# Turning the second tile's keys and queries behind the second product, not around it

## The chip, the core and the metric

The kernel runs on one core of a Trainium2 chip. The metric is the device time of one execution in microseconds (us), lower is better. Times are medians of several executions; the profile is one execution, recorded by the hardware profiler.

## The reference

Local attention feeds two feed-forward layers. Only the first part matters here; cut to it:

```python
# q, k, v: 4 batches, 8 heads, 768 positions, 64 features; 8 memory keys and values per head
for c in range(24):                            # chunks of 32 queries, context 16 left, 8 right
    scores = q_c @ concat(mem_k, k_ctx).T / 8
    a = softmax(scores)
    out[:, :, c_start:c_end] = a @ concat(mem_v, v_ctx)
x = out as 3072 tokens x 512
x = softplus(x @ w_in) @ w_out                 # d_ff 2048
x = (x @ w_a) * (x @ w_b) @ w_o2               # d_ff 1536
```

## The kernel before

The 3072 tokens are eight tiles of 384. For each tile the kernel computes attention, then for each of 16 slices f of d_ff the product `ph` (x with a slice of w_in, `emit_h`, L539), the softplus (`emit_soft`: three ACT instructions L545 to L547 make `e`, DVE adds `g` at L549, `split` makes the high part `g_h` on ACT, L526, and the low part `g_l`, L529, on DVE in the first tile), and two slices later the product `px` with w_out (`emit_x1`, L562), which adds into the four banks acc0 to acc3. Each matrix product is done as three, of high and low halves. The second layer follows when all tiles are done.

The first tile is the place of the change. Its attention is done ahead (`blocks`, written out by the table ROUND). Weights come from HBM as raw 64-bit words by `fetch_to(n)`, which requests all raws up to number n on SP's queue (L101). Each is converted by `Weight`: `top` on ACT (L116), `value` on DVE (two instructions, L121 and L122), `high` on ACT (L127), `low` on DVE (L130). Raws 0 to 5 are converted within ROUND, the others within the slices of the first tile, two half steps at a time (`convert`).

The second tile's first attention unit needs its keys and queries with features on partitions. `Packed(1).load(half)` requests them in two halves of four heads (`kp`, 400 KB, `qp`, 384 KB, and 8 KB of memory keys), and `Packed(1).turn(i)`, four calls, turns a pair of heads each: PE multiplies with the identity into `ptk` (L287, bank acc{i}) and `ptq` (L293, one of the two "att" banks), ACT copies `ptk` to `kn` (L289), DVE copies `ptq` to `qn` (L295). The scores `sc` of the unit (L304, L305) read `kn` and `qn` and take the two "att" banks after them.

Everything in the first tile stands in the order in which the program writes it, on each engine. Within slice f the order is: `ph`, softplus with conversions, plan entries of slots up to 2f, `px` of slice f - 2, plan entries of slots up to 2f + 1:

```python
plan += [(at, -1, lambda i=i: packed[1].turn(i)) for i, at in enumerate(PACKED_AT)]
def att_at(slot):
    while plan and plan[-1][0] <= slot:
        plan.pop()[2]()
```

The scores of the second tile's first unit stand at slot 5, behind the first `px`.

Of the kernel before, what the change touches and what calls it, by code (L numbers as in the profile page):

```python
# [31 lines left out]
ROUND = ((2, "normal"), (4, "place"), (None, "top"), (0, "scores"), (1, "soft"), (None, "low"), (None, "value"),  # L32
         (2, "flip"), (3, "values"), (None, "high"))
EARLY_RAW = (2, 3, 4, 5, 6, 6)
PACKED_AT = (0, 0.1, 2, 2.1)
AHEAD = 6
FILL = {(2, "scores"): 1, (2, "flip"): 5, (3, "flip"): 4, (3, "values"): 1, (4, "scores"): 2, (4, "flip"): 1,
        (4, "values"): 1, (5, "scores"): 2, (5, "flip"): 1, (5, "values"): 1, (6, "flip"): 4, (6, "values"): 1,
# [2 lines left out]
ROUNDS_CV = 6  # L41
# [9 lines left out]
def attn_moe_moe2(ctx: ExitStack, tc: tile.TileContext, q, k, v, mem_k, mem_v,  # L51
# [85 lines left out]
    def fetch1(n):  # L137
        dst, f = uses[n]
        if dst is w1:
            fetch(w1, f, w_in[:, f * P:(f + 1) * P].rearrange("(k p) f -> p k f", p=P))  # L140
        else:
            fetch(w1o, f, w_out[f * P:(f + 1) * P, :])
# [357 lines left out]
    for i, unit in enumerate(units[UPT:]):  # L500
# [10 lines left out]
        if i % UPT == UPT - 1 and unit.u + 1 < len(units):  # L511
            turned = at + steps[0][0] - steps[-1][0]
            plan += [(turned + 1 + part, i, partial(loaded.fetch, unit.u // UPT + 1, part)) for part in range(KT)]
    plan += [(at, -1, lambda i=i: packed[1].turn(i)) for i, at in enumerate(PACKED_AT)]
    plan.sort(key=lambda p: p[:2])
# [311 lines left out]
    def order():  # L827
# [6 lines left out]
        def fetch_to(n):  # L834
            nonlocal n_w1
            while n_w1 < min(n, len(uses)):
                fetch1(n_w1)
                n_w1 += 1
# [5 lines left out]
        for i in range(BPT):  # L844
            blocks[i].load()
            fetch_to(EARLY_RAW[i])
        packed[1] = Packed(1)
        packed[1].load(0)
        fetch_to(ROUNDS_CV + 2)
        packed[1].load(1)  # L850
        fetch_to(ROUNDS_CV + AHEAD)
        weights = [Weight(*use) for use in uses]
# [141 lines left out]
        while jobs:  # L994
# [6 lines left out]
            else:  # L1001
                next_job()

    order()


# [28 lines left out]
```

## Time and profile before

| what | value |
|---|---|
| median of 3 executions | 1189.81 us (1187.59 to 1191.05) |
| profiled execution | 1187.76 us |
| its span, first to last instruction | 1185.7 us |
| PE (matmul) busy | 1177.1 us, 99% |
| DVE busy, ACT busy | 734.8 us (62%), 536.7 us (45%) |

The profiled execution's time is 2.06 us over its span. PE is busy nearly all of the span, DVE and ACT over the whole kernel are not; in the first 100 us they are busy 81.03 and 80.98 us of it.

### The profile page before, as it was taken

The page shows a single profiled execution, that of the slowest core. Times are in us where ns is not written, and L with a number is a line of the kernel's source. Part 1 is how long each engine was busy: PE and PEld are TensorE (multiplying, and loading weights), DVE is VectorE, ACT ScalarE, POOL GpSimd, SP SyncE. Part 2 cuts the span into 40 slices and gives each one's busy share as a digit, 9 for nine tenths or more (in the row PEclk, how much of TensorE's full clock was granted, in tenths as well). Part 3 has the DMA queues.
Part 4 walks back from the last instruction along what each step waited for, and adds up shares of the span by engine and source line. Part 5 has one row for each costly group of instructions (what it writes and reads, how often), then busy time and mean ns, then how long its engine had stood idle before and what let it go on. Part 6 is the DMA issues. An engine that isn't in the chain of part 4 may idle for free.

```text
span 1185.7 us, 21520 instructions
## 1 busy us (share of the span) xinstructions
PE 1177.1 (99%) x7966; PEld 1115.3 (94%) x7966; DVE 734.8 (62%) x1707; ACT 536.7 (45%) x1329; POOL 279.2 (24%) x249
## 2 busy tenths in 40 slices
PE   9999999999999999999999999999999999999998
PEld 7899999999999999999999999999999999999997
DVE  6888654555546555465387668755666456655565
ACT  6899665655656566565564433221112201212010
POOL 2000323223232222322325778200211002100000
PEclk9999999999999999999999999999999999999999
DMA  9955334353343533432556895788554965379521
GB/s 232 296 183 112 107 86 111 93 113 107 85 110 93 118 110 83 105 97 62 177 206 239 321 339 193 266 323 301 201 196 143 375 231 184 133 254 365 198 80 54
DMA packets 198841, 209.86 MB, mean 177 GB/s; under 512 B 121632, under 2 KB 150224, under 8 KB 198736
## 3 DMA queue, kind: packets, MB, share of 16 engines
q1 hardware_dynamic: 198352, 208.43, 54.8%
q8 instruction: 63, 1.03, 0.4%
q14 instruction: 42, 0.34, 0.1%
q0 software_dynamic: 384, 0.05, 0.0%
HBM read 158.11 MB, written 50.33 MB: 176 GB/s over the span
## 4 chain that ended last, share of the span: by engine, by line
PE 95%; DMA 2%; SPq 2%; ACT 0%; DVE 0%; issue 0%; DVEq 0%
PE px L562 23%; PE ph L539 22%; PE py L749 17%; PE pW L726 8%; PE pX L726 8%; PE pV L726 8%; PE pY L726 4%; PE pxa L476 2%; PE sc L429 1%; DMA kp<-in_k_dram 1%; DMA raw<-in_moe_w_in_dram 1%; SPq L330 1%; SPq L327 0%; SPq L101 0%; PE sc L304 0%
## 5 line engine op out<-in xcount | busy, mean ns | idle before, releaser
L539 PE MATMUL ph<-x,w 128*128 128x384 f32 x1536 | 289.9, 336 | 0.1
L539 PEld LDWEIGHTS ph<-x,w 128*128 128x128 f32 x1536 | 266.7, 188 | 2.5 <-issue 0.3
L749 PE MATMUL py<-w2o,c 128*128 128x512 f32 (+1 forms) x870 | 222.2, 392 | 0.0
L549 DVE SCALAR_TENSOR_TENSOR g<-ph,e 128x384 f32<-128x384 f32 x128 | 71.3, 557 | 206.3 <-ACT e L547 205.9
L749 PEld LDWEIGHTS py<-w2o,c 128*128 128x128 f32 x870 | 160.5, 188 | 25.3
L808 ACT CAST c<-c 128x384 fp32r<-128x384 f32 x48 | 24.7, 514 | 302.5 <-DVE c L806 269.8
L726 PE MATMUL pX<-x,u 128*128 128x384 f32 x576 | 115.5, 334 | 0.0
L758 DVE TENSOR_TENSOR y<-py,y 128x512 f32<-128x512 f32 (+1 forms) x121 | 83.0, 686 | 47.4 <-PE py L749 46.9
L545 ACT ACTIVATE e<-ph 128x384 f32<-128x384 f32 x128 | 62.2, 486 | 104.0 <-PE ph L539 90.0
L726 PEld LDWEIGHTS pX<-x,u 128*128 128x128 f32 x576 | 102.1, 188 | 4.1
L447 DVE STREAM_TRANSPOSE af<-sm 32x256 f32<-32x256 f32 x180 | 78.2, 435 | 2.5
L804 DVE TENSOR_TENSOR d<-pW,q 128x384 f32<-128x384 f32 x48 | 26.7, 557 | 68.5 <-PE pW L726 68.5
L546 ACT ACTIVATE e<-e 128x384 f32<-128x384 f32 x128 | 67.3, 526 | 4.0
L547 ACT ACTIVATE e<-e 128x384 f32<-128x384 f32 x128 | 67.3, 526 | 3.8
L383 ACT ACTIVATE sm<-sm,st 128x96 f32<-128x96 f32 x168 | 60.5, 362 | 3.6 <-DVE st L379 3.6
L818 ACT CAST c<-c 128x384 fp32r<-128x384 f32 x48 | 24.6, 513 | 77.9 <-DVE c L816 76.9
L726 PE MATMUL pW<-xs,u 128*128 128x384 f32 x288 | 57.8, 335 | 0.0
L726 PE MATMUL pV<-xx,u 128*128 128x384 f32 x288 | 57.8, 335 | 0.0
L726 PE MATMUL pV<-xs,u 128*128 128x384 f32 x288 | 57.6, 334 | 0.0
L726 PE MATMUL pW<-xx,u 128*128 128x384 f32 x288 | 57.6, 334 | 0.0
L726 PE MATMUL pY<-xs,u 128*128 128x384 f32 x288 | 57.6, 334 | 0.0
L726 PEld LDWEIGHTS pV<-xx,u 128*128 128x128 f32 x288 | 51.5, 188 | 4.2
(251 smaller groups left out, 2228.9 us busy)
## 6 DMA issues: line engine op xcount, KB each, us to landing
u<-u_scratch SPq DMA_DIRECT2D x108, 512.0 KB
u_scratch<-u SPq DMA_DIRECT2D x36, 512.0 KB
w2o<-w2o_scratch SPq DMA_DIRECT2D x36, 512.0 KB
u<-u_scratch SPq DMA_DIRECT2D x36, 256.0 KB
raw<-in_moe_w_in_dram SPq DMA_DIRECT2D x16, 512.0 KB
raw<-in_moe_w_out_dram SPq DMA_DIRECT2D x16, 512.0 KB
vn<-in_v_dram SPq DMA_DIRECT2D x35, 176.0 KB
raw_a<-in_moe_w_a_dram SPq DMA_DIRECT2D x12, 512.0 KB
```

Source lines behind the costliest of these rows:

```text
L383: nc.scalar.activation(sm[:, h], sm[:, h], AF.Exp, bias=st[:, 0, h:h + 1], scale=-1.0, accum_out=st[:, 1, h:h + 1])
L447: nc.vector.transpose(out=af[32 * kb:32 * kb + 32, x], in_=self.sm[32 * x:32 * x + 32, :, 32 * kb:32 * kb + 32])
L539: nc.tensor.matmul(ph, lhsT=a, rhs=c, start=n == 0, stop=n == 3 * KT - 1)
L545: nc.scalar.activation(e, ph, AF.Abs)
L546: nc.scalar.activation(e, e, AF.Exp, scale=-1.0)
L547: nc.scalar.activation(e, e, AF.Ln, bias=1.0)
L549: nc.vector.scalar_tensor_tensor(g, ph, 0.0, e, ALU.max, ALU.add)
L562: nc.tensor.matmul(acc[t][i][:, :TT], lhsT=a, rhs=c, start=f == 0 and m == 0, stop=f == NF1 - 1 and m == 2)
L726: nc.tensor.matmul(bank[:, :TT], lhsT=u[:, j, a, kt * P:kt * P + P], rhs=x[:, c, kt, :], start=first_ and m == 0, stop=m == 3 * KH - 1, sk ...
L749: nc.tensor.matmul(b, lhsT=c[:, x, r], rhs=w[:, y, cols], start=n == 0, stop=n == 3 * GROUP - 1)
L758: tt(y, b, y, ALU.add)
L804: tt(d21, w[:, :TT], q, ALU.add)
```

## The change

The four turns move from slots 0, 0.1, 2, 2.1 to 2, 2.1, 3, 3.1. A turn with a fractional slot is taken at the next whole one: before, the first two stood at slots 0 and 1, between the first and the second `ph`, and the others at slots 2 and 3, between the second and the third. Now the first stands at slot 2 and the next two at slot 3, between the second and the third `ph`, and the fourth at slot 4, behind the third. The requests of raws 6 and 7 are put ahead of the first half's keys and queries, and that of raw 8 ahead of the second half's.

```diff
-PACKED_AT = (0, 0.1, 2, 2.1)
+PACKED_AT = (2, 2.1, 3, 3.1)
...
         for i in range(BPT):
             blocks[i].load()
             fetch_to(EARLY_RAW[i])
+        fetch_to(ROUNDS_CV + 2)
         packed[1] = Packed(1)
         packed[1].load(0)
-        fetch_to(ROUNDS_CV + 2)
+        fetch_to(ROUNDS_CV + 3)
         packed[1].load(1)
         fetch_to(ROUNDS_CV + AHEAD)
```

On PE, from the first tile's first `ph` on (ptk_0 and ptq_0 are the first turn, ptk_3 and ptq_3 the fourth), the program before had this:

```order
L539 MATMUL ph_0_623<-x_429,w_320 128x384 x12
L287 MATMUL ptk_0_673<-ident,kp_0_173 64x104 x8
L293 MATMUL ptq_0_683<-ident,qp_0_174 64x128 x6
L287 MATMUL ptk_1_691<-ident,kp_0_173 64x104 x8
L293 MATMUL ptq_1_701<-ident,qp_0_174 64x128 x6
L539 MATMUL ph_1_709<-x_429,w_368 128x384 x12
L287 MATMUL ptk_2_747<-ident,kp_1_183 64x104 x8
L293 MATMUL ptq_2_757<-ident,qp_1_184 64x128 x6
L287 MATMUL ptk_3_769<-ident,kp_1_183 64x104 x8
L293 MATMUL ptq_3_779<-ident,qp_1_184 64x128 x6
L539 MATMUL ph_2_787<-x_429,w_424 128x384 x12
```

Now it has this, with the first `px` next in both:

```order
L539 MATMUL ph_0_623<-x_429,w_320 128x384 x12
L539 MATMUL ph_1_673<-x_429,w_368 128x384 x12
L287 MATMUL ptk_0_711<-ident,kp_0_177 64x104 x8
L293 MATMUL ptq_0_721<-ident,qp_0_178 64x128 x6
L287 MATMUL ptk_1_733<-ident,kp_0_177 64x104 x8
L293 MATMUL ptq_1_743<-ident,qp_0_178 64x128 x6
L287 MATMUL ptk_2_751<-ident,kp_1_185 64x104 x8
L293 MATMUL ptq_2_761<-ident,qp_1_186 64x128 x6
L539 MATMUL ph_2_769<-x_429,w_424 128x384 x12
L287 MATMUL ptk_3_806<-ident,kp_1_185 64x104 x8
L293 MATMUL ptq_3_816<-ident,qp_1_186 64x128 x6
```

The second product has moved ahead of the first two turns, and the fourth turn behind the third product.

On DVE, from the low half of weight 8 on (tmp is the value of a raw, w the low half of a weight), the program before had this:

```order
L130 TENSOR_TENSOR w_670<-tmp_650,w_670 128x512
L295 COPY qn<-ptq_0_683 128x384
L295 COPY qn<-ptq_1_701 128x384
L121 TENSOR_SCALAR tmp_727<-raw_193 128x512
L122 SCALAR_TENSOR_TENSOR tmp_727<-raw_193,tmp_727 128x512
L549 SCALAR_TENSOR_TENSOR g_1_734<-ph_1_709,e_1_730 128x384
L130 TENSOR_TENSOR w_736<-tmp_663,w_736 128x512
L529 TENSOR_TENSOR g_1l<-g_1_734,g_1h 128x384
L121 TENSOR_SCALAR tmp_744<-raw_195 128x512
L122 SCALAR_TENSOR_TENSOR tmp_744<-raw_195,tmp_744 128x512
L295 COPY qn<-ptq_2_757 128x384
L295 COPY qn<-ptq_3_779 128x384
```

Now it has this:

```order
L130 TENSOR_TENSOR w_670<-tmp_650,w_670 128x512
L121 TENSOR_SCALAR tmp_691<-raw_193 128x512
L122 SCALAR_TENSOR_TENSOR tmp_691<-raw_193,tmp_691 128x512
L549 SCALAR_TENSOR_TENSOR g_1_698<-ph_1_673,e_1_694 128x384
L130 TENSOR_TENSOR w_700<-tmp_663,w_700 128x512
L529 TENSOR_TENSOR g_1l<-g_1_698,g_1h 128x384
L121 TENSOR_SCALAR tmp_708<-raw_195 128x512
L122 SCALAR_TENSOR_TENSOR tmp_708<-raw_195,tmp_708 128x512
L295 COPY qn<-ptq_0_721 128x384
L295 COPY qn<-ptq_1_743 128x384
L295 COPY qn<-ptq_2_761 128x384
L130 TENSOR_TENSOR w_786<-tmp_691,w_786 128x512
```

Five steps (a value, g of slice 1, a low half, its low part g_1l, a value) have moved ahead of the first copy of a turn. The fourth copy, qn from ptq_3, now stands behind this piece, which follows the last row above:

```order
L130 TENSOR_TENSOR w_786<-tmp_691,w_786 128x512
L549 SCALAR_TENSOR_TENSOR g_2_793<-ph_2_769,e_2_789 128x384
L121 TENSOR_SCALAR tmp_796<-raw_636 128x512
L122 SCALAR_TENSOR_TENSOR tmp_796<-raw_636,tmp_796 128x512
L529 TENSOR_TENSOR g_2l<-g_2_793,g_2h 128x384
L130 TENSOR_TENSOR w_803<-tmp_708,w_803 128x512
```

Before, no copy stood behind those rows; the softmax of the unit followed them, as it now follows the fourth copy.

On SP's queue, behind the last load of the first tile's values, the requests before were these (raw_179 is raw 6, raw_181 raw 7, raw_189 raw 8, raw_191 raw 9):

```order
L274 DMA kp_0_173<-in_k_dram 100x4x256
L275 DMA kp_0_173<-in_mem_k_dram 2x4x256
L276 DMA qp_0_174<-in_q_dram 128x4x192
L101 DMA raw_179<-in_moe_w_in_dram 128x4x256
L101 DMA raw_181<-in_moe_w_out_dram 128x1024
L274 DMA kp_1_183<-in_k_dram 100x4x256
L275 DMA kp_1_183<-in_mem_k_dram 2x4x256
L276 DMA qp_1_184<-in_q_dram 128x4x192
L101 DMA raw_189<-in_moe_w_in_dram 128x4x256
L101 DMA raw_191<-in_moe_w_out_dram 128x1024
```

Now they are these (raws 6, 7 and 8 are raw_173, raw_175 and raw_183):

```order
L101 DMA raw_173<-in_moe_w_in_dram 128x4x256
L101 DMA raw_175<-in_moe_w_out_dram 128x1024
L274 DMA kp_0_177<-in_k_dram 100x4x256
L275 DMA kp_0_177<-in_mem_k_dram 2x4x256
L276 DMA qp_0_178<-in_q_dram 128x4x192
L101 DMA raw_183<-in_moe_w_in_dram 128x4x256
L274 DMA kp_1_185<-in_k_dram 100x4x256
L275 DMA kp_1_185<-in_mem_k_dram 2x4x256
L276 DMA qp_1_186<-in_q_dram 128x4x192
L101 DMA raw_191<-in_moe_w_out_dram 128x1024
```

Raws 6 and 7 now stand ahead of both halves, raw 8 between them, and raw 9 where it was.

## Rows read from the trace of the kernel before

**Rows 1.** The page: busy time by engine; granted clock in tenths, 40 slices.

```profile
PE 1177.1 (99%) x7966; PEld 1115.3 (94%) x7966; DVE 734.8 (62%) x1707; ACT 536.7 (45%) x1329; POOL 279.2 (24%) x249
...
PEclk9999999999999999999999999999999999999999
```

**Rows 2.** Waits of PE over the whole span, all there are: us, times, longest.

```profile
PE pat L355 <- ACT x L369: 2.6, 3, 1.3
PE fill L492 <- POOL mem_n L228: 1.3, 1, 1.3
PE ptq L293 <- DVE qn L295: 1.0, 1, 1.0
```

**Rows 3.** Timeline of PE, 37 to 55 us: start, us, what, [idle before <-releaser].

```profile
37.06 2.64 PE L539 MATMUL ph<-x,w 128*128 128x384 f32 x12
...
39.63 0.93 PE L287 MATMUL ptk<-ident,kp 104*64 104x104 f32 x16
...
42.53 2.36 PE L539 MATMUL ph<-x,w 128*128 128x384 f32 x12
...
44.81 0.93 PE L287 MATMUL ptk<-ident,kp 104*64 104x104 f32 x16
...
46.77 0.88 PE L293 MATMUL ptq<-ident,qp 128*64 128x128 f32 x12 [1.02 <-DVE qn L295]
...
47.48 0.89 PE L287 MATMUL ptk<-ident,kp 104*64 104x104 f32 x16
...
48.95 2.35 PE L539 MATMUL ph<-x,w 128*128 128x384 f32 x12
...
53.31 0.40 PE L304 MATMUL sc<-kn,qn 64*64 64x88 f32 x8
...
54.56 2.35 PE L539 MATMUL ph<-x,w 128*128 128x384 f32 x12
```

**Rows 4.** Timeline of ACT, 40 to 52 us.

```profile
40.74 0.71 ACT L116 ACTIVATE raw<-raw 128x512 f32<-128x512 f32 x1 [1.49 <-DMA raw<-in_moe_w_in_dram]
...
41.87 0.47 ACT L545 ACTIVATE e<-ph 128x384 f32<-128x384 f32 x1
...
43.36 0.66 ACT L116 ACTIVATE raw<-raw 128x512 f32<-128x512 f32 x1
...
51.34 0.49 ACT L545 ACTIVATE e<-ph 128x384 f32<-128x384 f32 x1
```

**Rows 5.** Timeline of DVE, 37 to 56 us.

```profile
37.38 0.42 DVE L121 TENSOR_SCALAR tmp<-raw 128x512 uint32<-128x512 uint32 x1
...
38.51 0.42 DVE L121 TENSOR_SCALAR tmp<-raw 128x512 uint32<-128x512 uint32 x1
...
43.49 0.56 DVE L549 SCALAR_TENSOR_TENSOR g<-ph,e 128x384 f32<-128x384 f32 x1 [0.70 <-ACT e L547]
...
45.56 0.69 DVE L130 TENSOR_TENSOR w<-tmp,w 128x512 fp32r<-128x512 f32 x1
...
46.16 1.01 DVE L295 COPY qn<-ptq 128x384 f32<-128x384 f32 x2
...
47.10 0.42 DVE L121 TENSOR_SCALAR tmp<-raw 128x512 uint32<-128x512 uint32 x1
...
50.97 1.02 DVE L295 COPY qn<-ptq 128x384 f32<-128x384 f32 x2
...
55.66 0.25 DVE L379 CUSTOM_DVE_ANT_0 sm<-sc,mask 128x96 f32<-128x96 f32 x1
```

**Rows 6.** Window 40 to 42 us: busy PE, PEld, DVE, ACT, POOL, PEclk, DMA share, GB/s.

```profile
40.00:42.00 2.00, 2.00 (x48) 2.00 (x45) 1.27 (x3) 1.26 (x3) 0.00 (x0) 1.00 1.10 377
```

**Rows 7.** Timeline of PE, 0 to 31 us.

```profile
1.29 3.78 PE L492 MATMUL fill<-mem_n 128*128 128x512 f32 x4 [1.29 <-POOL mem_n L228]
...
27.84 1.13 PE L492 MATMUL fill<-ident 128*128 128x512 f32 x2
...
30.28 0.61 PE L355 MATMUL pat<-ident,work 128*96 128x128 f32 x4 [1.31 <-ACT x L369]
```

## The prediction

> **What bounds the kernel now.** I read the page first: PE is busy 99% of the span and its granted clock is full in every slice [rows 1]. So the time is PE's work plus PE's waits, and a change that adds no matmuls can move the end only through the waits. The list of PE's waits is the second view: it has three lines, and the last one, 1.0 us on a copy of the turned queries, is the only one within the change [rows 2]. No later wait is listed. The reader should see two things in this. At most about 1 us can be won here. And whatever PE loses before about 55 us it cannot win back, because behind that point no wait is left to shorten; a shift there goes through to the end.
>
> The third view is PE's timeline. From 39.63 PE does turns 0 and 1, the second `ph` from 42.53, turn 2's keys from 44.81, and then stands 1.02 us before turn 2's queries (46.77) until the copy of turn 0's queries has freed an "att" bank; `ph` number three starts at 48.95, the scores at 53.31, the fourth `ph` at 54.56 [rows 3]. I measure the change by the start of that fourth `ph`, since the same work stands ahead of it in both programs.
>
> Last, why that copy was late. ACT stood 1.49 us for raw 8, which landed at 40.74 [rows 4]; DVE's copies began only at 46.16, behind a low half begun at 45.56 [rows 5]. DVE takes its instructions in program order, so the place of a copy in its order is what counts.
>
> **The change, part by part.**
>
> *Requests.* Raw 8 no longer stands behind the second half of keys and queries. That half is 400 + 384 + 8 = 792 KB, and the transfers ran at 377 GB/s around the landing with the engines fully busy [rows 6], so raw 8 lands 2.15 us earlier (an estimate: 792 x 1024 bytes at that rate), at 38.6. ACT's wait then goes. What replaces it is DVE's own work: from 37.38 it does three values and two low halves before g of slice 0. A value takes 1.13 us (38.51 - 37.38), a low half 0.60 (46.16 - 45.56) [rows 5], so g starts at 37.38 + 3 x 1.13 + 2 x 0.60 = 41.97, not 43.49: 1.52 earlier. ACT is no later: from e's first step to g there are 1.62 us (41.87 to 43.49) [rows 4, 5], and without its wait that step comes at least 1.49 earlier, at 40.38 or before, so ACT allows g at 42.00. Raw 9 keeps its place in the bytes. It must be there by 42.4 for the value behind g; after raw 8's old landing one raw of 512 KB takes 1.4 us at the same rate, so 42.1. The trace only proves 43.36, where ACT took it without a wait [rows 4]; that bound costs 0.9 us more. The second half lands where raw 8 used to, at 40.74, and is first turned at 44.81 or later: hidden, with 4 us to spare. If that cover were gone, each us of lateness beyond it would be a us of PE. SP is not late with anything else: raw 9 and those behind it keep their places.
>
> *PE's order ahead of the first wait.* The second `ph` and turns 0 and 1 change places. They are the same instructions, so PE stands at 44.81 with the same work done, does turn 2's keys, and comes to turn 2's queries at 45.75 in both programs. The move itself costs nothing there.
>
> *First wait: the copy of turn 0's queries.* Before, from g of slice 0 to that copy there were 2.67 us (43.49 to 46.16). Now five more steps stand ahead of it: a value, g of slice 1, a low half, g_1l and a value. The same five stand between the two pairs of copies before, and took from 47.10 to 50.97, 3.87 us [rows 5]. So the copy starts at 41.97 + 2.67 + 3.87 = 48.51, which is 2.35 later than 46.16. PE followed the copy's start by 0.61 (46.16 to 46.77) [rows 3, 5], so turn 2's queries start at 49.12: a wait of 3.37 in place of 1.02. Queued behind it on PE are the third `ph`, turn 3, the first `px` and the scores, and with the third `ph` ACT's and DVE's slice 2. **First term: +2.35.** If raw 8's earlier landing gave nothing, it would be +2.35 + 1.52 = +3.87.
>
> *Second wait: the copy of turn 3's queries.* It now stands on DVE behind g of slice 2, a value, g_2l and a low half, all of which wait for the third `ph`, and the scores need it. After turn 2's queries (0.71, 46.77 to 47.48) the third `ph` starts. Count from there. PE needs 4.36 us for that `ph` and the `px` (48.95 to 53.31) and 1.45 for turn 3 (half of 39.63 to 42.53), so it could begin the scores at 5.81 [rows 3]. ACT begins on the `ph` at 2.39 (48.95 to 51.34) [rows 3, 4]; from there to the end of that chain of DVE's, where the softmax began before, are 4.32 us (51.34 to 55.66) [rows 4, 5], and the copy and its release take 0.61. So the scores are released at 2.39 + 4.32 + 0.61 = 7.32. **Second term: 7.32 - 5.81 = +1.51.** An ACT copy of turn 3's keys holds the last part of `px` in the meantime, since it stands behind ACT's share of slice 2; it lies within this wait and is not counted again. The lower bound of the term is 0, if the chain were hidden; it can't be less, as PE's own work is only moved.
>
> **Sum.** 2.35 + 1.51 = +3.86 us, on PE, with nothing behind to absorb it. Relative to the scores the softmax is even earlier than before (DVE is done with the low half that held it to 55.66), so slices 3 and on are not held up further. Against the profiled execution: 1187.76 + 3.86 = 1191.6. The median of the runs shown is 2.05 above that execution; the changed kernel's time will be a median too, so I give 1189.81 + 3.86 = 1193.7.
>
> **Clock.** The longest stretch that PE stood before, once it had begun, is 1.31 us [rows 7], and the granted clock is full in all slices [rows 1]; by these rows a wait leaves no trace on the clock. They show no wait as long as 3.37 us, however. If the clock fell to its lower level of 1.2 GHz there, turn 2's queries and the third `ph` (0.71 + 2.28 = about 3.0 us) could take up to twice as long, so the price is between 0 and +3.0. That matmuls do run slower when PE has been idle is in the trace: the first four of 512 columns took 3.78 us, two of the same size later 1.13 [rows 7], which is 0.95 against 0.57 each. I take 0, the nearer row being the 1.31 us wait. The Trainium skill, "TensorE: Matmul & The Clock Gate", section "HAM oscillation — how this bites in real kernels", speaks against this choice: a wait between groups of matmuls lets the array be throttled to half rate again, so that the next group starts slow. By it the sum would be nearer to +6.9, by the rows +3.86; no run here yet shows which.
>
> **The rivals.**
>
> *The clock falls in the long wait* (chance 0.12): +3.86 + 3.0 = +6.9, 1196.7. For it: 3.37 us is more than twice any earlier wait. Against: the full clock throughout.
>
> *The earlier raw 8 gives nothing* (0.12), because the transfers ahead of it are held by something else than bytes, or raw 9 takes its place as the late one: +1.52 more at most, +5.4, 1195.2. For it: 43.36 is all that is proven for raw 9. Against: the transfer engines are full, so bytes ahead decide.
>
> *Only the first wait costs* (0.14): the chain behind the third `ph` is shorter than I read, for instance because the conversions are already done: +2.35, 1192.2, within a measurement's reach of no change.
>
> *Not slower* (0.04): the copies come in time and only the relief remains. If turn 0's copy still stood right behind weight 8's low half, it would start at 41.97 + 2.67 = 44.64 and PE's wait would be gone: -1.02, 1188.8. It decides if the copy starts at 46.16 - 1.02 = 45.14 or before. For it: the chain of ACT, DVE and the landing that made the wait does get shorter. Against: the order puts 3.87 us of DVE's work ahead of the copy, and DVE had no gap in those rows to do it in earlier.
>
> **How the numbers follow.** My forecast, both waits and a full clock, has 0.58. The likeliest time is 1193.7. A measurement of this kernel can tell about 0.3%, or 3.57 us, from no change; the three runs shown spread over 3.5 us. The forecast is only just above that, so I split its 0.58 into 0.37 slower and 0.21 same. The clock and the raw 8 rivals are slower (0.24), the one-wait rival is same (0.14), and the not-slower rival is same but for 0.03 with scatter. Faster 0.03, same 0.36, slower 0.61. The range goes from the one-wait rival, with scatter, at 1190 to the clock rival at 1197; it leaves out the not-slower rival and the tails of the others, about 0.15.
>
> **What the profile after should show.** No wait of ACT for raw 8. PE's wait before `ptq` on a DVE copy at 3.4 us instead of 1.0, beginning near 45.75. A second, new wait of about 1.5 us of PE on the copy before the scores, part of it perhaps charged to `px` and ACT. The fourth `ph` at about 58.4 instead of 54.56, and from there the same pace to the end. Full clock in the slice at 46 to 60 us; a lower figure there means the clock rival. I am wrong if the copy of turn 0's queries starts before 46, if PE shows waits on `kp` or `qp` transfers, or if the fourth `ph` is late and the end is not.

## The result, and the profile after

The changed kernel takes 1194.94 us (median of 8 executions, 1193.44 to 1196.61), the kernel before 1189.45 (8, 1187.09 to 1193.52). The ratio is 1.0051, with a 95% interval of 1.0036 to 1.0065: slower by half a per cent. The profiled execution took 1193.52 us, 5.76 more than that of before, with a span of 1191.4.

The page's lines that answer to [rows 1]:

```profile
PE 1178.9 (99%) x7966; PEld 1116.4 (94%) x7966; DVE 735.1 (62%) x1707; ACT 537.1 (45%) x1329; POOL 279.4 (23%) x249
...
PEclk9999999999999999999999999999999999999999
```

PE's work is nearly the same. The clock's line shows nothing, but it could not show a short fall: each digit is an average over 30 us, and a 9 stands for 90% or more. All waits of PE, to be read beside [rows 2]:

```profile
PE ptq L293 <- DVE qn L295: 4.0, 1, 4.0
PE pat L355 <- ACT x L369: 2.7, 3, 1.3
PE fill L492 <- POOL mem_n L228: 1.3, 1, 1.3
PE px L562 <- ACT kn L289: 0.5, 1, 0.5
PE ptk L287 <- issue: 0.4, 1, 0.4
```

The wait before `ptq` has grown from 1.0 to 4.0 us, and a wait of `px` on ACT's copy of turn 3's keys is new. PE's timeline, beside [rows 3]:

```profile
37.44 4.72 PE L539 MATMUL ph<-x,w 128*128 128x384 f32 x24
...
42.09 0.93 PE L287 MATMUL ptk<-ident,kp 104*64 104x104 f32 x16
...
49.77 0.88 PE L293 MATMUL ptq<-ident,qp 128*64 128x128 f32 x12 [4.01 <-DVE qn L295]
...
50.58 3.92 PE L539 MATMUL ph<-x,w 128*128 128x384 f32 x12
...
54.43 0.94 PE L287 MATMUL ptk<-ident,kp 104*64 104x104 f32 x16
...
58.25 0.44 PE L562 MATMUL px<-g_0h,w 128*128 128x384 f32 x1 [0.47 <-ACT kn L289]
...
59.45 0.41 PE L304 MATMUL sc<-kn,qn 64*64 64x88 f32 x8
...
60.64 2.36 PE L539 MATMUL ph<-x,w 128*128 128x384 f32 x12
...
62.84 0.33 PE L562 MATMUL px<-g_1h,w 128*128 128x384 f32 x1
```

The first `ph` starts 0.38 us later than in the profile before, which is scatter ahead of the change, so I count from it: to the fourth `ph` there were 54.56 - 37.06 = 17.50 us, and there are 60.64 - 37.44 = 23.20. That is +5.70, and the whole span grew by 5.7. The third `ph` (50.58) is 3.92 us long, where it was 2.35. What the other engines did, ACT first, beside [rows 4]:

```profile
39.53 0.68 ACT L116 ACTIVATE raw<-raw 128x512 f32<-128x512 f32 x1
...
42.23 0.69 ACT L116 ACTIVATE raw<-raw 128x512 f32<-128x512 f32 x1
```

and DVE, beside [rows 5]:

```profile
37.76 0.42 DVE L121 TENSOR_SCALAR tmp<-raw 128x512 uint32<-128x512 uint32 x1
...
42.49 0.55 DVE L549 SCALAR_TENSOR_TENSOR g<-ph,e 128x384 f32<-128x384 f32 x1
...
49.17 1.02 DVE L295 COPY qn<-ptq 128x384 f32<-128x384 f32 x2
...
58.85 0.55 DVE L295 COPY qn<-ptq 128x384 f32<-128x384 f32 x1
```

ACT takes raw 8 at 39.53 and raw 9 at 42.23, neither with a wait. DVE's g of slice 0 comes at 42.49, but the first two copies only at 49.17. Last, the windows around the long wait (columns as in [rows 6]; the third figure from the end is the granted clock):

```profile
46.00:48.00 2.00, 0.00 (x0) 0.00 (x0) 2.00 (x4) 1.68 (x5) 0.00 (x0) 1.00 0.75 216
48.00:50.00 2.00, 0.23 (x4) 0.23 (x6) 1.90 (x5) 1.81 (x5) 0.00 (x0) 1.00 0.61 113
50.00:52.00 2.00, 2.00 (x16) 1.83 (x13) 1.34 (x3) 0.00 (x0) 0.00 (x0) 0.66 0.91 290
52.00:54.00 2.00, 2.00 (x8) 2.00 (x8) 0.00 (x0) 0.00 (x0) 0.00 (x0) 0.50 0.98 310
54.00:56.00 2.00, 2.00 (x32) 1.57 (x30) 0.00 (x0) 1.40 (x3) 0.00 (x0) 0.99 0.93 323
```

PE does nothing from 46 to 48 us and almost nothing to 50, and the granted clock is 0.66 and then 0.50, the lower of its two levels, just when the third `ph` runs; by 54 to 56 us it is back. If the clock stood only at 1.00 or 0.50 in between, the means of 0.66 and 0.99 put the fall at about 50.6 us, 0.9 us after PE had begun again, and the rise at about 54.0 (estimates from these windows).

### The profile page after: what moved, and what is told of

The parts are those of the page before. It is cut to its first block, busy times and chain, and to the rows that moved or that the text cites. A ratio compares the mean times of both kernels' runs of the same rounds, so it can differ in the third digit from the quotient of the medians.

```text
span 1191.4 us, 21520 instructions
## 1 busy us (share of the span) xinstructions
PE 1178.9 (99%) x7966; PEld 1116.4 (94%) x7966; DVE 735.1 (62%) x1707; ACT 537.1 (45%) x1329; POOL 279.4 (23%) x249
## 4 chain that ended last, share of the span: by engine, by line
PE 95%; DVE 1%; DMA 1%; ACT 1%; SPq 0%; issue 0%; DVEq 0%; ACTq 0%
PE px L562 23%; PE ph L539 22%; PE py L749 17%; PE pW L726 8%; PE pX L726 8%; PE pV L726 8%; PE pY L726 4%; PE pxa L476 2%; PE sc L429 1%; DMA raw<-in_moe_w_in_dram 1%; DVE tmp L122 1%; DMA vv<-in_v_dram 0%; ACT work L383 0%; DVE w L130 0%; ACT w L127 0%
```

## The experiments

The theory: the loss has three parts, all from the turns' new place. DVE comes late to turn 0's copy (first wait); the clock falls on account of that wait; DVE comes late to turn 3's copy (second wait). The moved requests are a small relief. The rivals: the requests cost; the order on PE costs; the third `ph` is slow for another reason. The kernels ran in three groups, each beside the kernel before on the same chip; its medians there were 1187.82 us (17 executions), 1188.94 (35) and 1189.02 (26).

**Only the requests.**

```diff
-PACKED_AT = (2, 2.1, 3, 3.1)
+PACKED_AT = (0, 0.1, 2, 2.1)
```

> The turns stay at their old slots and only the requests are moved. Theory (the loss is the place of the turns, and the requests alone are a small relief): ACT no longer waits 1.49 us for raw 8, the copy of turn 0's queries starts at about 44.6 instead of 46.16, PE's wait of 1.02 us before turn 2's queries goes, the fourth ph starts at about 53.5 instead of 54.56 and the time is 1.0 us (0.09%) under the kernel before. Rival (the moved requests are part of the loss, because the second half of keys and queries or raw 9 lands late): a wait of PE or ACT on a transfer appears and the time is 1 us or more over the kernel before.

Measured: 1187.23 against 1187.82, ratio 0.9993 (0.9979 to 1.0007). The 0.6 us under the kernel before have the expected sign, but are not clear of zero. ACT's timeline, then PE's:

```profile
39.16 0.68 ACT L116 ACTIVATE raw<-raw 128x512 f32<-128x512 f32 x1
...
43.06 0.68 ACT L116 ACTIVATE raw<-raw 128x512 f32<-128x512 f32 x1 [1.11 <-DMA raw<-in_moe_w_out_dram]
```
```profile
46.05 0.88 PE L293 MATMUL ptq<-ident,qp 128*64 128x128 f32 x12 [0.31 <-DVE qn L295]
...
53.86 2.35 PE L539 MATMUL ph<-x,w 128*128 128x384 f32 x12
```

Raw 8 is taken without a wait, at 39.16, and the fourth `ph` is 0.70 us earlier than in [rows 3]. But raw 9 is now late by 1.11 us, so that the wait before `ptq` shrinks to 0.31 and does not vanish. In this order of the turns the requests are no part of the loss.

**Only the turns.** The same two lines the other way, in the kernel before.

> The turns are at their new slots and the requests as before. Theory: raw 8 lands at 40.7 again, ACT's wait of 1.5 us is back and everything on DVE comes 1.2 to 1.5 us later than with the whole change, so PE's wait before turn 2's queries is about 5.3 instead of 4.0 and the time is 6.7 to 7.5 us over the kernel before (0.6%). Rival (the requests cost): the wait is 4.0 or less and the time at most 5.5 us over.

Measured: 1197.31, ratio 1.0077 (1.0063 to 1.0090): 9.5 us over, more than either expectation, on the theory's side. ACT, then PE:

```profile
42.52 0.71 ACT L116 ACTIVATE raw<-raw 128x512 f32<-128x512 f32 x1 [2.57 <-DMA raw<-in_moe_w_in_dram]
```
```profile
52.54 1.55 PE L293 MATMUL ptq<-ident,qp 128*64 128x128 f32 x12 [6.45 <-DVE qn L295]
...
54.02 4.09 PE L539 MATMUL ph<-x,w 128*128 128x384 f32 x12
```

In this execution ACT waited 2.57 us for raw 8, where it waited 1.49 in the profile before, so raw 8 was 1.1 us later against the work around it. PE's wait is 6.45 us, 2.44 more than in the whole change, where ACT did not wait for raw 8. The clock was low as well: the queries take 1.55 us and the third `ph` 4.09.

**The long wait filled.** In the whole change, in the turn's code:

```diff
+            if t and i == 2:
+                warm(12)
             for r in range(3):
```

> The whole change, and three products of the identity with itself, 512 columns each, on PE between turn 2's keys and turn 2's queries, that is in the long wait; their result is not used. Theory (the third ph took 3.9 us in place of 2.35 because the clock was at its lower level after the wait): the granted clock stays full from 46 to 56 us, the third ph takes 2.4 us, and of the loss of 5.5 us some 1.7 go: 3.8 us over the kernel before, 0.32%. The wait itself ends at the same time. Rival (the third ph is slow for another reason, such as transfers that run beside it): it takes 3.9 us again and the time is the whole change's, 5.5 us over.

Measured: 1193.53, ratio 1.0047 (1.0032 to 1.0061), 5.7 over in place of 3.8. PE's timeline and a window:

```profile
49.00 0.88 PE L295 MATMUL ptq<-ident,qp 128*64 128x128 f32 x12 [1.33 <-DVE qn L297]
...
49.80 2.36 PE L541 MATMUL ph<-x,w 128*128 128x384 f32 x12
...
58.30 2.37 PE L541 MATMUL ph<-x,w 128*128 128x384 f32 x12
```
```profile
50.00:52.00 2.00, 2.00 (x12) 1.84 (x11) 1.07 (x2) 0.00 (x0) 0.00 (x0) 1.00 0.91 300
```

The mechanism is as expected: the idle part of the wait is 1.33 us, the clock stays at 1.00 and the third `ph` takes 2.36 us. From the first `ph` (36.54) to the fourth are 21.76 us, 1.44 less than in the whole change. The median did not follow. The six executions took from 1191.26 to 1195.14; the two with a mean granted clock of 1.000 took 1191.3, or 3.5 over, and in the other four the clock was 0.998 or 0.999, so it fell in them in spite of the fill. So I repeated the pair on one chip:

> The whole change once more, so that the next runs have it on the same chip. Theory: 5 to 6 us over the kernel before, granted clock 0.996 to 0.999 in every execution.

> The whole change with three products of the identity in the long wait, as before, now beside the whole change on one chip. Theory (the clock is worth 1.4 to 1.7 us, and the median of the first comparison was moved by executions in which raw 9 landed late): 1.0 to 1.8 us under the whole change. Rival (the clock is not what costs): within 0.5 us of the whole change.

Measured: the whole change 1194.14 (9 executions, ratio 1.0042, 1.0025 to 1.0059), 5.1 us over with a mean clock of 0.995 to 0.999, and with the fill 1192.41 (12, ratio 1.0029, 1.0017 to 1.0042). That is 1.73 us less, what the theory asked for, though the intervals overlap, and in five of the twelve the mean clock was still 0.998 or 0.999. The whole change's own profile fell on an execution of 1197.17 us, and shows what made this one long; ACT, then PE:

```profile
45.06 0.67 ACT L116 ACTIVATE raw<-raw 128x512 f32<-128x512 f32 x1 [2.40 <-DMA raw<-in_moe_w_out_dram]
```
```profile
52.09 1.55 PE L293 MATMUL ptq<-ident,qp 128*64 128x128 f32 x12 [6.66 <-DVE qn L295]
```

Raw 9 landed 2.40 us after ACT was ready for it, and PE's wait was 6.66 us.

**All four turns ahead of the third `ph`.**

```diff
-PACKED_AT = (2, 2.1, 3, 3.1)
+PACKED_AT = (2, 2.1, 2.9, 3)
```

> The whole change, but turn 3 too stands between the second and the third ph. Theory (the copy of turn 3's queries behind slice 2's chain on DVE costs 1.3 to 1.5 us before the scores): the copy now stands right behind the other three, PE's waits on ACT's copy of turn 3's keys and before the scores go, PE's long wait stays at 4.0, and the time is 1.3 to 1.5 us under the whole change, 4.1 us over the kernel before (0.35%). Rival (that wait is only a shadow of something later on DVE or ACT): the time is the whole change's, 5.5 us over, with a wait elsewhere before 70 us.

Measured: 1193.76 against 1187.82, ratio 1.0046 (1.0034 to 1.0058): 5.9 us over, not 4.1. PE's timeline and windows:

```profile
49.95 1.55 PE L293 MATMUL ptq<-ident,qp 128*64 128x128 f32 x12 [4.00 <-DVE qn L295]
...
56.72 0.33 PE L562 MATMUL px<-g_0h,w 128*128 128x384 f32 x1
```
```profile
48.00:50.00 2.00, 0.05 (x2) 0.05 (x2) 1.90 (x5) 1.48 (x4) 0.00 (x0) 0.56 0.71 185
50.00:52.00 2.00, 2.00 (x22) 2.00 (x24) 0.81 (x2) 0.00 (x0) 0.00 (x0) 0.50 0.89 285
52.00:54.00 2.00, 2.00 (x24) 1.76 (x20) 0.10 (x1) 1.02 (x2) 0.00 (x0) 0.50 1.03 376
54.00:56.00 2.00, 2.00 (x10) 1.91 (x9) 1.16 (x2) 0.00 (x0) 0.00 (x0) 0.73 1.06 381
```

PE's list has no wait on ACT's copy of keys or before the scores any more: the second wait is gone, and the first is unchanged. The time is not 1.3 us lower: from `ptq` at 49.95 to the first `px` at 56.72 are 6.77 us, where the rest of turn 2, turn 3 and a `ph` take 4.36 at the full clock (0.71 and 1.45 by [rows 3], and 2.20 from 60.64 to 62.84 above). So 2.4 us go to the low clock now, against some 1.7 in the whole change. The windows show why: by the same estimate as above the clock fell at about 48.2 us, 1.7 before PE began again, and rose at about 55.1. After a wait of the same length it was low during some 5.1 us of PE's work here, and 3.4 in the whole change. No run shows what sets the moment of the fall.

**Both together:** the four turns as here, and a fill of `warm(16)`.

> The whole change with turn 3 too ahead of the third ph and with four products of the identity, 512 columns each, in the long wait; their result is not used. Theory (first wait, second wait and clock are the three parts of the loss): only the first wait is left, 4.0 us filled with work that nothing needs, so the time is 2.6 to 3.2 us over the kernel before, the clock full in most executions, and they spread less than those of the whole change. Rival (the parts don't add up, or the clock falls anyway): 4 us or more over.

Measured: 1191.26, ratio 1.0026 (1.0014 to 1.0037), 2.3 us over, just under the expectation; ten of twelve executions had a clock of 1.000. PE in the profiled one:

```profile
51.72 0.88 PE L295 MATMUL ptq<-ident,qp 128*64 128x128 f32 x12 [2.43 <-DVE qn L297]
```

PE still stood 2.43 us behind the fill, at a full clock; ACT had waited 2.43 us for raw 9 in this execution. With the second wait and, in most executions, the low clock taken away, what is left is the first wait.

**The copies first.** The four turns behind the second `ph` on PE, but written ahead of slice 1's conversions and softplus:

```diff
-    plan += [(at, -1, lambda i=i: packed[1].turn(i)) for i, at in enumerate(PACKED_AT)]
...
             for f in range(NF1):
                 ph = emit_h(t, f)
+                if (t, f) == (0, 1):
+                    for i in range(KT):
+                        packed[1].turn(i)
                 if t == 0:
```

> The changed requests; all four turns on PE between the second and the third ph, as the change means it, but written ahead of slice 1's softplus, so that on DVE and ACT their copies stand right behind weight 8 and ahead of slice 1's value, g, low half and g_1l. Theory (the loss is the copies' place on DVE; that the turns stand behind the second ph on PE costs nothing): no wait of PE over 0.5 us before turn 2's queries, a full clock, and a time like that of the requests alone, 0.0 to 1.0 us under the kernel before. Rival (the order on PE is what costs, since the second half of keys and queries is turned before the third ph): 3 us or more over the kernel before, with PE waiting for the copies as in the whole change.

> The requests as before; the four turns on PE between the second and the third ph with their copies right behind weight 8 on DVE. Theory: the same work in front of the same wait, so within 1 us of the kernel before. Rival (the order on PE costs): 3 us or more over.

Measured: with the changed requests 1189.28 against 1188.94, ratio 1.0003 (0.9993 to 1.0013), and with the old requests 1190.21, ratio 1.0010 (0.9996 to 1.0023). They are 0.3 and 1.3 us over, both a little above what was expected and neither clear of zero. DVE and PE with the changed requests:

```profile
45.16 1.01 DVE L295 COPY qn<-ptq 128x384 f32<-128x384 f32 x2
```
```profile
45.77 0.88 PE L293 MATMUL ptq<-ident,qp 128*64 128x128 f32 x12
...
53.56 2.35 PE L538 MATMUL ph<-x,w 128*128 128x384 f32 x12
```

All four turns stand between the second and the third `ph` on PE, and no wait is left before `ptq` or the scores. The fair comparison is the run above with all four turns ahead of the third `ph`: it has the same order on PE and the same requests, and only the copies' place on DVE and ACT differs. That run was 5.9 us over the kernel before and this one is 0.3, each against the kernel before on its own chip. Not all that is won up to the fourth `ph` reaches the end: it follows the first `ph` (37.44) by 16.12 us, 1.38 less than before, but behind it the span is 1.6 us longer than in the profile before (1186.3 - 53.56 against 1185.7 - 54.56), and PE's list has 0.7 us of new waits there, on ACT's copies for the attention units that follow (`pxa`). The second kernel's profile, ACT, PE and a window:

```profile
41.67 0.70 ACT L116 ACTIVATE raw<-raw 128x512 f32<-128x512 f32 x1 [2.52 <-DMA raw<-in_moe_w_in_dram]
```
```profile
47.69 1.17 PE L293 MATMUL ptq<-ident,qp 128*64 128x128 f32 x12 [2.39 <-DVE qn L295]
...
48.63 1.60 PE L287 MATMUL ptk<-ident,kp 104*64 104x104 f32 x16
```
```profile
48.00:50.00 2.00, 2.00 (x28) 2.00 (x24) 0.65 (x2) 0.00 (x0) 0.00 (x0) 0.53 0.72 171
```

With the old requests ACT waited 2.52 us for raw 8 in that execution, and PE 2.39 us for the copy; after that wait the clock fell, and the keys' turn at 48.63 takes 1.60 us instead of 0.89.

**Raw 9 earlier,** in the whole change:

```diff
-        fetch_to(ROUNDS_CV + 3)
+        fetch_to(ROUNDS_CV + 4)
         packed[1].load(1)
```

> The whole change with raw 9 too requested ahead of the second half of keys and queries. Theory (raw 9 became the late one in many executions, by up to 2.4 us, and the part of the loss that the sum doesn't have is this): 0.5 to 1.5 us under the whole change, ACT without a wait for raw 9. Rival (raw 9 is hidden by DVE's own work): within 0.3 us of the whole change.

Measured: 1194.70, ratio 1.0047 (1.0029 to 1.0064), 0.6 us above the whole change on the same chip and not under it. The theory of this run falls. ACT in its profile:

```profile
41.78 0.69 ACT L116 ACTIVATE raw<-raw 128x512 f32<-128x512 f32 x1
...
45.41 0.68 ACT L116 ACTIVATE raw<-raw 128x512 f32<-128x512 f32 x1 [1.76 <-DMA raw<-in_moe_w_in_dram]
```

Raw 9 is taken at 41.78 without a wait, and then raw 10 is 1.76 us late: in this execution the change of order only moved the lateness from one raw to the next, and PE's wait was 5.64 us.

**A version to beat both:** turns 0 and 1 behind the second `ph`, 2 and 3 behind the third, each pair ahead of its slice's softplus.

```diff
-    plan += [(at, -1, lambda i=i: packed[1].turn(i)) for i, at in enumerate(PACKED_AT)]
...
                 ph = emit_h(t, f)
+                if t == 0 and f in (1, 2):
+                    for i in (2 * f - 2, 2 * f - 1):
+                        packed[1].turn(i)
```

It has raw 9 ahead of the second half as well, and once it ran with the requests of before.

> A version meant to be better than both: turns 0 and 1 behind the second ph and turns 2 and 3 behind the third, each pair's copies ahead of that slice's softplus on DVE and ACT, and raw 9 too requested ahead of the second half. Theory (what is left are ACT's wait for raw 9, 1.1 us in the run with the requests alone, and PE's 0.3 us for the second half's queries): no wait of ACT for a raw, no wait of PE between the second and the fourth ph, 1.0 us under the kernel before, and fewer slow executions. Rival (DVE and ACT are late whatever lands, so a wait of PE before the scores takes its place): no better than the requests alone.

> The turns and copies as in the better version, spread over two slices, with the requests of the kernel before. Theory (PE's 1.0 us wait and the slow executions of the kernel before come from raw 8's landing, and the place of the turns gives little by itself): 0 to 0.7 us under the kernel before and 1 us over the better version, with executions as scattered as those of the kernel before. Rival (the place of the turns is what gives): 1.5 us under the kernel before, as the better version.

Measured: 1187.27 against 1188.94, ratio 0.9985 (0.9975 to 0.9994), and with the old requests 1188.51 against 1189.02, ratio 0.9996 (0.9984 to 1.0009). The gain of the new place and the requests together, raw 9's included, is 1.7 us and clear of zero; the gains of the new place alone, 0.5 us here, and of the requests alone, above, are not, though the intervals overlap. PE in the better version:

```profile
36.66 4.74 PE L538 MATMUL ph<-x,w 128*128 128x384 f32 x24
...
52.94 2.35 PE L538 MATMUL ph<-x,w 128*128 128x384 f32 x12
```

No wait of PE is left there, ACT waits for no raw, and the fourth `ph` starts 16.28 us after the first (52.94 - 36.66, against 17.50). With the old requests, ACT and PE:

```profile
42.78 0.70 ACT L116 ACTIVATE raw<-raw 128x512 f32<-128x512 f32 x1 [3.63 <-DMA raw<-in_moe_w_in_dram]
```
```profile
46.13 2.36 PE L538 MATMUL ph<-x,w 128*128 128x384 f32 x12 [1.56 <-DVE g L548]
```

ACT waited 3.63 us for raw 8, and PE stood only 1.56 for it, before the third `ph`, at a full clock. The scatter that was expected did not come: none of these twelve executions took more than 1189.99 us, while eight of the 26 of the kernel before took 1191.29 or more.

## Why the prediction held, and which term was missed

The prediction's range and sign held, and both waits came where it put them. That the time fell inside the range is in part luck: the forecast had a full clock, and its +3.86 us is two thirds of the 5.76 that the profiles differ by. Most of the rest is a term that the sum put at 0, and the range held it because it reached up to the clock rival. By the prediction's own steps:

*Requests.* Right: ACT's wait for raw 8 went, and g of slice 0 came 4.73 us after DVE's first value (37.76 to 42.49), where 4.59 were worked out. That raw 9 would be there at 42.1 held in the profiled execution, but not in others (2.40 us late above); the 0.9 us given as its bound was too small.

*First wait.* Right in place and kind, a little short in size. Counted from the first `ph`, turn 2's queries start after 12.33 us (49.77 - 37.44) in place of 9.71 (46.77 - 37.06): +2.62 for +2.35, since the copy started 11.41 us after DVE's first value in place of 11.13. The wait itself grew more, by 2.99 us (4.01 - 1.02), because PE came to it 0.37 us earlier than I let it: two `ph` in a row, for instance, took 4.65 us (37.44 to 42.09), not the 4.85 that they took apart.

*Second wait.* Right: from the third `ph`'s end to the fourth's start there were 6.21 us (54.43 to 60.64) for 4.86 of work (1.45 for the turn, 4.36 - 2.20 for `px`, 1.25 for the scores), +1.35 where +1.51 stood. As said, part is charged to `px` and ACT.

*Clock.* Here the sum failed: "I take 0, the nearer row being the 1.31 us wait". The third `ph` held PE 3.85 us (50.58 to 54.43) where the fourth held it 2.20: +1.65, inside the bounds of 0 and +3.0 that were kept for the range. The fill shows that it is the clock, as the same `ph` takes 2.36 us when PE is kept busy in most of that wait. The rival with the clock, given 0.12, was the one that came, at half its price. Its evidence against was weak: "the full clock throughout" was read from a line that shows nines in the changed kernel too. Nor did the slow first products of [rows 7] speak for the low clock: the windows of the profile before have 1.00 from 0 to 6 us, so the record does not tie their 0.95 us to the clock. The Trainium skill, "TensorE: Matmul & The Clock Gate", section "HAM oscillation — how this bites in real kernels", says that a wait between groups of matmuls lets the array be throttled again. By that rule the trace agrees, with 0.50 in the window of 52 to 54 us.

The three make 2.62 + 1.35 + 1.65 = 5.62, and turn 2's queries hold PE 0.10 longer (49.77 to 50.58 in place of 0.71); the profile has 5.70. Against its own time I had 1191.6 and the profiled execution took 1193.52: the miss is 1.9, of which the clock is 1.65. Nearly all of the shift went through to the end, as argued from the list of waits: from the fourth `ph` to the end of the span there are 1130.8 us (1191.4 - 60.64), where there were 1131.1.

*The other rivals.* That the requests give nothing, or that raw 9 takes raw 8's place as the late one, is wrong in the first profile of the whole change and true in the second, where ACT waited 2.40 us for raw 9 and PE 6.66. "Only the first wait" is refuted by the timeline, with +1.35 behind the third `ph`. "Not slower" needed the copies to stand where they stood; the run with the copies first made it so, and is level with the kernel before.

What stays open is why the transfers land late in some executions. The same requests as before had ACT wait for raw 8 1.49, 2.57, 2.52 and 3.63 us in four profiles. That the scatter of the kernel before comes from this is likely and not shown: of its 35 executions in the second comparison eleven took 1190.07 us or more, each at a mean clock of 0.998 or 0.999, and none of the better version's twelve took more than 1188.80. A late raw 8 alone does not explain it, since with the new place of the turns and the old requests raw 8 was late in the profile too and no execution was long.

## What to carry to other kernels

On engines that work in program order, a step moved on PE drags its copies with it on the others; look up what then stands ahead of the copy there, and add it up, before asking whether PE's order is better. Place the copies first and the conversions, which nothing awaits soon, behind them. When a sum makes PE wait longer than any wait the profile shows, give the clock a price of its own, as a range worked out from the matmuls that stand behind the wait; here it came to 1.65 and to 2.4 us behind waits of the same length.

## What the runs showed of the hardware

In the profiles of runs without a fill the granted clock fell to its lower level, 0.50, after waits of PE of 2.39, 4.00, 4.01, 5.64, 6.45 and 6.66 us, and stayed at 1.00 after 1.56 us and less; behind a fill it stayed at 1.00 through waits of 1.33, 1.51 and 2.43 us. These are single profiles, and in some executions with a fill the mean clock was below 1.000 as well.

The fall does not come at a fixed place. In the whole change the clock was still 1.00 in the windows in which PE stood idle, and fell about 0.9 us after PE had begun again; with all four turns ahead of the third `ph` it fell about 1.7 us before PE began. Both waits were 4.0 us long, and the prices were 1.65 and 2.4 us, as the low clock covered some 3.4 and 5.1 us of PE's work. So the price of such a wait is a range and not one number; what decides within it, no run here shows.
